# The second chunk's C product as seven block products, with its state sums made by accumulating transfers

## The chip, the cores and the metric

The kernel runs on one core of a Trainium2 chip. The time is the device time of one execution in microseconds (us). The kernel before took 206.87 us (median of three runs, 206.71 to 207.6). The engines are named as in the profile: PE is the tensor engine, DVE the vector engine, ACT the scalar engine, POOL is GpSimd and SP the sync engine, which only issues transfers here. POOL's transfers can add to their destination; SP's can only copy or transpose.

## The reference, cut to what matters

Two branches run on the same input `x` (2048 tokens x 640) and a gate mixes them:

```python
g = sigmoid((x * gate_w).sum(-1, keepdims=True))
# branch a: a diagonal complex state-space layer with 640 states
h_t = Lam_bar * h_(t-1) + x_t B_bar                  # a scan over the 2048 tokens
a   = 2 * (h Cmat).real + x * Dskip                  # the C product
# branch b: a dense layer pair
b   = gelu(x w1 + b1) w2 + b2                        # 640 -> 1728 -> 640
out = g * a + (1 - g) * b
```

The C product multiplies the real and the imaginary part of 640 states, so 1280 numbers a token, with a matrix of 1280 x 640.

## The kernel before

The 2048 tokens are four chunks of 512 (`CH`), and a chunk is four tiles of 128 tokens (`TPC`). Each chunk passes through four stages.

- `ff1(c)` makes x w1 + b1 and its gelu. PE fills a PSUM bank with five matmuls of 512 columns (line 305) and ACT evicts it into `gel[c]` (line 314).
- `ssm(c)` makes the input of the scan, x B: five matmuls of 512 columns for each of ten banks (line 481), which ACT evicts into `bu` buffers (line 484, eight buffers). DVE then runs, for each of the five groups of 128 states, a rotation (three operations of 128 x 1024), two scans (line 575), a rotation back (three operations, line 557) and writes the states into `hs[c]`. Between two chunks ACT turns the end states into the next start (`turn_carry`, four small activations, line 590).
- `fin_b(c)` is the w2 product. It is made as a product of 2 x 2 blocks with seven block products in place of eight (Strassen's scheme, in Winograd's form): tokens are halved, the 1728 inner rows are halved, and the 640 columns are halved. PE multiplies, and ACT copies a partial result to a second bank where two results share a first part (`fork`, line 744). ACT also scales each result by the gate into the f32 tiles `gb` (`out_of`, line 752). The sums of gelu blocks that the scheme needs are made by ACT's negated copies (`minus`, line 682) and POOL's accumulating transfers (`plus`, line 677). One product, Q, goes into both halves of a row of tiles; `twice` sends it from an f32 buffer `gq` (two buffers) with an accumulating transfer.
- The C product comes last and gives the output. Chunks 0 and 1 have it in the plain form, `fin_a` (line 812): for each of four tiles and two column halves, ten matmuls of 320 columns, 80 in all. The term x * Dskip is put into the bank by ACT before (`seed`, line 668), and one DVE operation (line 817) multiplies by the gate and adds `gb`. Chunks 2 and 3 have it as seven block products, `fin_s` (line 877): the tokens, the states (real and imaginary half) and the columns are halved, and seven products of two tiles and five matmuls make 70 matmuls. Its steps are X (first product), a copy X to Y, the Q product, then Y, X (with copies to Z and W) and Z. ACT makes the copies (line 883) and evicts Q into `gq` (line 920). DVE adds the skip term into `gb` (`skip_in`, lines 859 and 861), Q (`part_7`, line 904) and makes the outputs (`done`, line 892). For chunks 2 and 3 DVE also makes the four sums of state blocks (`h_sums`, line 836) into `M7`, `hs` itself, `M6` and `M3`. The sums of blocks of the matrix C (`U4` to `U7`) are made once, during `ff1(3)`, by ACT and POOL.

Seven products need the sums of states: with the blocks a, b (first half of the tokens) and g21, d (second half), M7 = a - g21, g21 becomes g21 + d, M6 = a - (g21 + d), M3 = b + M6.

The order on PE, ACT, POOL and SP is the order of the calls at the end of the kernel (lines 973 to 1015), with further work hung in by dictionaries of hooks. On DVE the order is made by a small planner: operations wait in a list and are let out by estimated times of PE, ACT and DVE (`dve_now`, `let_out`, `ck`). All engines run their lists in order, so an operation that waits holds up all that stand behind it. From chunk 1 on the calls are:

```python
gates(1); load_xT(2); load_skip(); fin_b(0, ...)
ff1(2, ...); gates(2); fin_a(0, sums(1)); load_xT(3)
ssm(2, ...); fin_b(1, ...); fin_a(1, ...); ssm(3)
ff1(3, ...); gates(3); fin_b(2, ...); fin_s(2, ...); fin_b(3, ...); fin_s(3, ...)
```

PSUM has eight banks, and `gel`, `hs`, `gq` and `g` have two buffers each.

Of the kernel before, what the change touches and what calls it, by code (L numbers as in the profile page):

```python
# [16 lines left out]
P = 128  # L17
# [25 lines left out]
def kernel(  # L43
# [41 lines left out]
    xT = [xA, xB, xB, xA]  # L85
# [12 lines left out]
    CT_im = const.tile([P, KS, D], BF16, name="CT_im")  # L98
    TCOS = const.tile([P, KS, CH], BF16, name="TCOS")
# [77 lines left out]
    tfi = work.tile([P, HC], I32, name="e", bufs=1)  # L177
    nc.gpsimd.iota(tfi[:], pattern=[[1, HC]], base=0, channel_multiplier=0)
# [8 lines left out]
    tf = const.tile([P, NP], F32, name="tf")  # L187
# [72 lines left out]
    nc.vector.tensor_copy(out=tf[:, NQ:NP], in_=tfi[:])  # L260
# [105 lines left out]
    scr = gelp.tile([P, KF * CH // 2], F32, name="gel")  # L366
# [21 lines left out]
    kk = work.tile([P, KS, NP], I32, name="bu", bufs=8)  # L388
# [27 lines left out]
    nc.vector.tensor_tensor(out=u, in0=tf[:].rearrange("p (o i) -> p o i", o=1).to_broadcast([P, KS, NP]), in1=over(thp_c[:], NP), op=ALU.mult)  # L416
# [59 lines left out]
    def inputs(c, ks):  # L476
        bu = work.tile([P, 2, CH], BF16, name="bu", bufs=8)
        for ri, BT in enumerate((BT_re, BT_im)):
            p = bank()
            for kd in range(KD):  # L480
                nc.tensor.matmul(p[:], lhsT=BT[ks >= KSA][:, kd, (ks % KSA if ks < KSA else ks - KSA) * P:][:, 0:P], rhs=xT[c][:, kd, :],  # L481
                                 start=(kd == 0), stop=(kd == KD - 1))
                pe(CH)
            nc.scalar.activation(out=bu[:, ri, :], in_=p[:], func=ACT.Identity)  # L484
            act(0.6)
        return bu, ck.act
# [157 lines left out]
    def gates(c):  # L644
        sl = slice(c * TPC, (c + 1) * TPC)

        def f():
            nc.vector.tensor_scalar(out=gcol[:, 0, sl], in0=gz[:, sl], scalar1=0.5, scalar2=0.5, op0=ALU.mult, op1=ALU.add)
            nc.vector.tensor_scalar(out=gcol[:, 1, sl], in0=gz[:, sl], scalar1=-0.5, scalar2=0.5, op0=ALU.mult, op1=ALU.add)
            nc.vector.tensor_scalar(out=gcol[:, 2, sl], in0=gz[:, sl], scalar1=0.5, scalar2=-0.5, op0=ALU.mult, op1=ALU.add)  # L650

        dve_now(ck.act + 0.3 if c > 0 else ck.pe, 0.2, f)
# [68 lines left out]
    def fin_b(c, at={}, gs=None):  # L721
# [59 lines left out]
        fork("X", "Z")  # L781
        if c < NCH - 1:
            part_7()
# [46 lines left out]
    U5, U7, U6, U4 = (narrow(t, KS * HD).rearrange("p (k d) -> p k d", k=KS) for t in (BT_re[1][:], BT_im[1][:], xB[:], w1b_sb[:]))  # L830
    M6, M7 = (t[:].rearrange("p k t -> p (k t)").rearrange("p (k t) -> p k t", k=KS) for t in (BT_im[0], BT_re[0]))
    M3 = narrow(xA[:], KS * HT).rearrange("p (k t) -> p k t", k=KS)
    C11, C12, C21, C22 = (t[:, :, h * HD:(h + 1) * HD] for t in (CT_re, CT_im) for h in range(2))

    def add(out, x, y, op):
        return lambda: nc.vector.tensor_tensor(out=flat(out), in0=flat(x), in1=flat(y), op=op)

    def h_sums(c):
        (a, b), (g21, d) = ([hs[c][:, i, r] for r in range(2)] for i in range(2))
        steps = []  # L840
        for out, x, y, op in ((M7, a, g21, ALU.subtract), (g21, g21, d, ALU.add), (M6, a, g21, ALU.subtract), (M3, b, M6, ALU.add)):
            steps.append(lambda fn=add(out, x, y, op): dve_now(0, 0.8, fn))
        return steps, (a, M7, M6, b, g21, M3, d), (C11, U7, U6, C21, U5, C22, U4)

    wide = [narrow(w1a_sb[:], 6 * D)[:, j * 2 * D:(j + 1) * 2 * D].bitcast(F32) for j in range(3)]
    wide += [xA[:].rearrange("p k t -> p (k t)")[:, KS * HT:].bitcast(F32), narrow(w1c_lo[:], 2 * D).bitcast(F32)]
# [8 lines left out]
    def skip_in(c, tiles, d0, d1, ready=0):  # L855
        for a in tiles:
            ti = c * TPC + a
            if a >= H:
                dve_now(ready, 0.82, lambda: nc.vector.tensor_tensor(out=gbs[ti][:], in0=gbs[ti][:], in1=GS[c][a - H], op=ALU.add))
                continue  # L860
# [4 lines left out]
    def fin_s(c, lhs, rhs, at={}):  # L865
# [104 lines left out]
    def sums(c):  # L970
# [17 lines left out]
    fin_a(0, sums(1))  # L988
    load_xT(3)
    ssm(2, {KS - 1: lambda: skips(1)})  # L990
    fin_b(1, seeds(1))
    fin_a(1, {**sums(2), 3: lambda: minus(U6, C22, 1.5)})
    ssm(3)
    gel_tile(3)
    nc.sync.dma_start(out=U7, in_=C12)
    steps, lhs, rhs = h_sums(2)
    ff1(3, 0, {1: lambda: (minus(U5, C11, 1.5), plus(U7, U6), plus(U5, C12), plus(U6, U5)),
               5: lambda: (skips(2), let_out(0, 2), [f() for f in steps[:3]]),
               7: lambda: (skips(2, H), [load_xn((NCH - 1) * TPC + H + j, narrow(w1a_sb[:], 6 * D)[:, (4 + j) * D:(5 + j) * D]) for j in range(H)]),
               10: lambda: (nc.sync.dma_start(out=U4, in_=C21), plus(U4, U6))})  # L1000
    for a, t in ((0, w1c_hi[:].rearrange("p k f -> p (k f)")[:, 0:D]), (1, xB[:].rearrange("p k t -> p (k t)")[:, KS * HD:KS * HD + D])):
        load_xn((NCH - 1) * TPC + a, t)
    gates(3)
    nc.vector.tensor_scalar(out=gcol[:, 3, NT - 2 * TPC:NT], in0=gcol[:, 0, NT - 2 * TPC:NT], scalar1=-1.0, scalar2=None, op0=ALU.mult)
# [4 lines left out]
    last, lhs3, _ = h_sums(3)  # L1009
    fin_s(2, lhs, rhs, {0: lambda: skip_in(2, (0, 1), HD, D, ck.act + 0.5), 1: lambda: (minus_d(3), skips(3))})  # L1010
    fin_b(3, {0: lambda: (let_out(1e9), [f() for f in last]),
# [3 lines left out]
    fin_s(3, lhs3, rhs)  # L1015
# [30 lines left out]
```

## Time and profile before

| | |
|---|---|
| time, median of three runs | 206.87 us |
| the profiled execution | 206.56 us, of which the span from first to last instruction is 204.8 us |
| PE busy | 200.6 us (98%), 1301 matmuls |
| DVE busy | 186.6 us (91%) |
| ACT busy | 140.7 us (69%) |
| POOL busy | 50.6 us (25%) |
| chain that ended last | PE 97% |
| granted PE clock | 1.00 throughout |

The span is the time from the first to the last instruction; the execution is 1.8 us longer. The chain that ended last is followed back from the last instruction: at each step to what released it, or to the instruction before it on its engine. A share of 97% for PE says that nearly all of the time one matmul followed another. The stages stand in that chain with their starts: `ssm(2)` at 94.9 us, `fin_b(1)` at 105.7, `fin_a(1)` at 119.2, `ssm(3)` at 130.1, `ff1(3)` at 140.9, `fin_b(2)` at 155.5, `fin_s(2)` at 168.8, `fin_b(3)` at 178.4 and `fin_s(3)` at 191.7. Timeline rows give the start of an instruction in us from the span's start, its duration, engine, line, operation and tiles; a bracket at the end is the idle time before it and what ended that.

### The profile page before, as it was taken

What the parts mean: (1) busy time and instruction counts of PE and PEld (TensorE: products, weight loads), DVE (VectorE), ACT (ScalarE), POOL (GpSimd) and SP (SyncE); (2) the same over time, 40 slices, a digit from 0 to 9 for tenths busy, and PEclk for the clock granted to TensorE, in tenths of its full rate; (3) what the DMA queues carried; (4) which work ended last, traced back from release to release, by engine and by line L of the source; (5) the groups of instructions that cost most, each with busy time, mean ns of one, the idle gap of its engine ahead of it and who ended that gap; (6) DMA issues with size and microseconds to landing.
All of it is one profiled execution on the core that took longest, in us unless ns stands there. A gap on an engine that the chain in (4) does not pass through costs nothing.

```text
span 204.8 us, 3592 instructions
## 1 busy us (share of the span) xinstructions
PE 200.6 (98%) x1301; PEld 119.3 (58%) x1301; DVE 186.6 (91%) x314; ACT 140.7 (69%) x271; POOL 50.6 (25%) x83
## 2 busy tenths in 40 slices
PE   8999999999999999999999999999999999999993
PEld 5744544454477544675457777544446777777762
DVE  2799999999999999999999999999999999686573
ACT  4696856997866799991764899266776699255520
POOL 8506930313330410031001052200412170124000
PEclk9999999999999999999999999999999999999999
DMA  6999999999999160159932369912596989719303
GB/s 192 193 144 223 194 303 158 203 224 287 177 210 219 23 109 15 50 104 239 194 90 53 74 120 234 235 35 80 89 190 121 182 159 198 175 24 208 60 0 128
DMA packets 45190, 30.28 MB, mean 148 GB/s; under 512 B 26898, under 2 KB 42612, under 8 KB 45172
## 3 DMA queue, kind: packets, MB, share of 16 engines
q0 software_dynamic: 6448, 12.53, 36.1%
q1 hardware_dynamic: 38148, 17.03, 35.5%
q10 hardware_dynamic: 576, 0.49, 0.7%
q8 instruction: 10, 0.16, 0.3%
q14 instruction: 8, 0.07, 0.1%
HBM read 7.79 MB, written 2.62 MB: 51 GB/s over the span
## 4 chain that ended last, share of the span: by engine, by line
PE 97%; DVE 1%; DVEq 0%; issue 0%
PE bank L305 28%; PE bank L732 26%; PE bank L481 21%; PE bank L812 11%; PE bank L877 9%; PE bank L264 1%; PE bank L329 1%; DVE ot L892 0%; PE bank L267 0%; DVE xA L274 0%; DVEq L1041 0%; PE bank L408 0%; PE bank L420 0%
## 5 line engine op out<-in xcount | busy, mean ns | idle before, releaser
L314 ACT ACTIVATE gel<-bank,colB 128x512 bf16<-128x512 f32 (+1 forms) x52 | 33.5, 692 | 7.9 <-PE bank L305 7.6
L575 DVE TENSOR_TENSOR_SCAN g<-r_c,carry,v 128x512 bf16<-128x512 f32 x30 | 38.3, 1277 | 0.0
L484 ACT ACTIVATE bu<-bank 128x512 bf16<-128x512 f32 x40 | 23.3, 600 | 19.3 <-PE bank L481 19.2
L732 PEld LDWEIGHTS <-gel 128*128 128x128 bf16 x280 | 27.3, 98 | 11.1 <-issue 0.2
L732 PE MATMUL bank<-w_sb,gel 128*128 128x320 bf16 x168 | 24.3, 299 | 0.0
L752 ACT ACTIVATE gb<-bank,gcol 128x320 f32<-128x320 f32 x32 | 16.2, 526 | 7.4 <-PE bank L732 6.9
L305 PEld LDWEIGHTS <-w1a_sb 128*128 128x128 bf16 x162 | 13.9, 98 | 12.0 <-issue 0.2
L812 PEld LDWEIGHTS <-hs 128*128 128x128 bf16 x160 | 15.6, 98 | 6.0
L481 PEld LDWEIGHTS <-BT_im 128*128 128x128 bf16 x100 | 9.7, 98 | 12.0 <-DMA BT_im<-in_A_B_im_dram 0.5
L481 PEld LDWEIGHTS <-BT_re 128*128 128x128 bf16 x100 | 9.6, 98 | 11.0
L744 ACT ACTIVATE bank<-bank 128x320 f32<-128x320 f32 x16 | 6.8, 423 | 11.0 <-PE bank L732 11.0
L305 PE MATMUL bank<-xA,w1a_sb 128*128 128x128 bf16 (+2 forms) x102 | 14.1, 291 | 0.0
L557 DVE TENSOR_TENSOR v<-wa,bu 128x1024 bf16<-128x1024 bf16 x20 | 13.7, 685 | 0.1
L557 DVE TENSOR_TENSOR hs<-wb,g 128x1024 bf16<-128x1024 bf16 x20 | 13.7, 685 | 0.1
L557 DVE TENSOR_TENSOR g<-TSIN,g 128x1024 bf16<-128x1024 bf16 x20 | 13.7, 685 | 0.1
L557 DVE TENSOR_TENSOR wb<-TCOS,g 128x1024 bf16<-128x1024 bf16 x20 | 13.7, 686 | 0.0
L557 DVE TENSOR_TENSOR bu<-TSIN,bu 128x1024 bf16<-128x1024 bf16 x20 | 13.6, 682 | 0.1
L812 PE MATMUL bank<-CT_re,hs 128*128 128x320 bf16 x80 | 13.5, 299 | 0.0
L812 PE MATMUL bank<-CT_im,hs 128*128 128x320 bf16 x80 | 13.5, 299 | 0.0
L732 PEld LDWEIGHTS <-N 128*128 128x128 bf16 x112 | 11.0, 98 | 4.3
L557 DVE TENSOR_TENSOR wa<-TCOS,bu 128x1024 bf16<-128x1024 bf16 x20 | 13.4, 670 | 0.0
L305 PEld LDWEIGHTS <-w1b_sb 128*128 128x128 bf16 x80 | 7.7, 98 | 9.6 <-DMA w1b_sb<-in_B_w_dram 0.7
(193 smaller groups left out, 398.1 us busy)
## 6 DMA issues: line engine op xcount, KB each, us to landing
out_dram<-ot SPq DMA_DIRECT2D x15, 160.0 KB, 5.0
w_sb<-in_B_w_dram SPq DMA_DIRECT2D x4, 480.0 KB, 5.7
gel<-N POOLq DMA_DIRECT2D x4, 448.0 KB, 4.9
N<-gel POOLq DMA_DIRECT2D x3, 448.0 KB, 5.6
gel<-gel POOLq DMA_DIRECT2D x3, 448.0 KB, 7.3
N<-N POOLq DMA_DIRECT2D x3, 448.0 KB, 5.2
gb<-gq POOLq DMA_DIRECT2D x4, 320.0 KB, 4.8
xn<-in_A_x_dram SPq DMA_DIRECT2D x8, 160.0 KB, 4.2
```

What stands on the lines that cost most here:

```text
L264: nc.tensor.matmul(pA[:, 0:n], lhsT=ones(P), rhs=ones(n), start=True, stop=True)
L305: nc.tensor.matmul(p[:, t0:t1], lhsT=w, rhs=xT[c][:, kd, t0:t1], start=(kd == 0) if first is None else first, stop=(kd == last), skip_grou ...
L314: nc.scalar.activation(out=dst, in_=src, func=ACT.Gelu_apprx_tanh, bias=b1_c[p0:p1, kf:kf + 1])
L481: nc.tensor.matmul(p[:], lhsT=BT[ks >= KSA][:, kd, (ks % KSA if ks < KSA else ks - KSA) * P:][:, 0:P], rhs=xT[c][:, kd, :], start=(kd == 0 ...
L484: nc.scalar.activation(out=bu[:, ri, :], in_=p[:], func=ACT.Identity)
L557: nc.vector.tensor_tensor(out=o, in0=a, in1=b, op=op)
L575: nc.vector.tensor_tensor_scan(s["g"][:, ri, :], r_c[:, ks:ks + 1].to_broadcast([P, CH]), s["v"][:, ri, :], init, ALU.mult, ALU.add)
L732: nc.tensor.matmul(p[:, 0:HD], lhsT=lhs[:, s, j * P:(j + 1) * P], rhs=rhs[:, s, :], start=fresh and s == 0, stop=s == KH - 1, skip_group_c ...
L744: nc.scalar.activation(out=quad[j][dst][:, 0:HD], in_=quad[j][src][:, 0:HD], func=ACT.Identity)
L752: nc.scalar.activation(out=gbs[ti][:, h * HD:(h + 1) * HD], in_=quad[j][name][:, 0:HD], func=ACT.Identity, scale=gcol[:, 1, ti:ti + 1])
L812: nc.tensor.matmul(p[:, 0:d1 - d0], lhsT=hs[c][:, a // H, j // KS, j % KS, (a % H) * P:][:, 0:P], rhs=CT[:, j % KS, d0:d1], start=False, s ...
L877: nc.tensor.matmul(t[j][:, d0:d1], lhsT=A[i][:, k, j * P:(j + 1) * P], rhs=B[i][:, k, d0:d1], start=fresh and k == 0, stop=k == KS - 1, sk ...
```

## The change

Chunk 1's C product becomes `fin_s(1)`: 70 matmuls in place of 80, the seven products, four bank copies of two, and two Q evictions on ACT. Its eight seeds on ACT go, and its skip term goes to `skip_in` on DVE (four operations of 320 columns, two of 640), with two `part_7`.

The state sums of chunk 1 are not made on DVE: `sum_7` and `sum_6` let ACT write -g21 into `M7` and `M6` (now tiles of their own) and let POOL add a, d and a to `M7`, `g21` and `M6`. `M3` of chunk 1 lies in the gelu buffer of chunk 1; SP copies b into it and POOL adds `M6`.

The sums of C's blocks are needed earlier. `U7` is C12 in place, to which POOL adds -C22 right after `fin_a(0)`. `U6` lies in `xA`: ACT writes -C22 there during `fin_a(0)` and, as the first operation of `fin_b(1)`, -C11; POOL then adds `U7`. `U5` and `U4` of chunk 1 lie in `N3` and `N2`, the buffers of `fin_b(1)`: SP copies C22 and C21 there when the products that read `N3` and `N2` are done, and POOL adds `U6` (and `M6` to `M3` in between). Chunks 2 and 3 get their `U5` and `U4` the same way in `ff1(3)`.

A new hook, `hook(4)`, stands in `fin_b` between the copy X to Z and `part_7`. The x of chunk 3 is loaded into `xB`, after `ssm(2)`, and no longer into `xA`. The `bu` buffers are six in place of eight. Two small tiles of the setup move into the scratch part of a gelu buffer. The fourth gate column is made in `gates` for chunks 1 to 3. The plain loads of chunk 2's x (`load_xn`) stand after `fin_s(1)`.

```diff
-    xT = [xA, xB, xB, xA]
+    xT = [xA, xB, xB, xB]
+    M6, M7 = (const.tile([P, KS, HT], BF16, name=n) for n in ("M6", "M7"))
...
-        bu = work.tile([P, 2, CH], BF16, name="bu", bufs=8)
+        bu = work.tile([P, 2, CH], BF16, name="bu", bufs=6)
...
+            if c > 0:
+                nc.vector.tensor_scalar(out=gcol[:, 3, sl], in0=gz[:, sl], scalar1=-0.5, scalar2=-0.5, op0=ALU.mult, op1=ALU.add)
...
         fork("X", "Z")
+        hook(4)
         if c < NCH - 1:
             part_7()
...
+    U7, U6 = C12, block(xA)
+    U54 = {1: (block(N3), block(N2)), 2: (block(BT_re[1]), block(BT_im[1]))}
+    U54[3] = U54[2]
+    def M3(c):
+        home = gel[1][:, 0, 0:KH, :] if c == 1 else xB[:]
+        return narrow(home, KS * HT).rearrange("p (k t) -> p k t", k=KS)
...
+    def sum_7():
+        (a, _), (g21, d) = state(1)
+        minus(M7[:], g21, 1.25)
+        plus(flat(M7[:]), flat(a))
+        plus(flat(g21), flat(d))
+
+    def sum_6():
+        (a, b), (g21, _) = state(1)
+        minus(M6[:], g21, 1.25)
+        plus(flat(M6[:]), flat(a))
+        nc.sync.dma_start(out=flat(M3(1)), in_=flat(b))
+
+    def sums_54(c, first=lambda: None):
+        U5, U4 = U54[c]
+        nc.sync.dma_start(out=U5, in_=C22)
+        nc.sync.dma_start(out=U4, in_=C21)
+        plus(U5, U6)
+        first()
+        plus(U4, U6)
...
-    fin_a(0, sums(1))
-    load_xT(3)
-    ssm(2, {KS - 1: lambda: skips(1)})
-    fin_b(1, seeds(1))
-    fin_a(1, {**sums(2), 3: lambda: minus(U6, C22, 1.5)})
-    ssm(3)
+    fin_a(0, {**sums(1), 3: lambda: minus(U6, C22, 1.5)})
+    plus(U7, U6)
+    ssm(2, {2: sum_7, KS - 1: lambda: (skips(1), skips(1, H))})
+    load_xT(3)
+    fin_b(1, {0: lambda: (minus(U6, C11, 1.5), plus(U6, U7)),
+              1: sum_6,
+              4: lambda: sums_54(1, lambda: plus(flat(M3(1)), flat(M6[:]))),
+              3: lambda: skip_in(1, (0, 1), 0, HD)})
+    fin_s(1, {0: lambda: skip_in(1, (0, 1), HD, D, ck.act + 0.5)})
+    for a in range(TPC):
+        load_xn(2 * TPC + a)
+    ssm(3, {1: lambda: minus_c(2), 3: lambda: minus_d(2)})
     gel_tile(3)
-    nc.sync.dma_start(out=U7, in_=C12)
...
-    ff1(3, 0, {1: lambda: (minus(U5, C11, 1.5), plus(U7, U6), plus(U5, C12), plus(U6, U5)),
+    ff1(3, 0, {1: lambda: sums_54(2),
```

## The prediction, made before the changed kernel ran

> **What bounds the kernel now.** I read the page first: busy shares, then the chain that ended last.
>
> ```profile
> span 204.8 us, 3592 instructions
> ...
> PE 200.6 (98%) x1301; PEld 119.3 (58%) x1301; DVE 186.6 (91%) x314; ACT 140.7 (69%) x271; POOL 50.6 (25%) x83
> ...
> PE 97%; DVE 1%; DVEq 0%; issue 0%
> ```
>
> PE is the bound: what takes a matmul away gains, and any idle PE is lost for good. Then the chain in order of time around the change:
>
> ```profile
> 105.70 1.90 PE bank L732 x14
> 107.60 0.02 issue
> 107.62 11.57 PE bank L732 x84
> 119.19 10.87 PE bank L812 x80
> ...
> 168.80 9.61 PE bank L877 x70
> ```
>
> 80 plain matmuls take 10.87, 70 block matmuls 9.61. And after the first 14 matmuls of `fin_b(1)` PE stood 0.02: it waited for the copy X to Y. So I read ACT's timeline there, then POOL's, the transfers' landing times, DVE's tail and PE's.
>
> ```profile
> 106.60 0.65 ACT L590 ACTIVATE carry<-e,e,cq 128x1 f32<-128x1 bf16 x2
> 107.16 0.90 ACT L744 ACTIVATE bank<-bank 128x320 f32<-128x320 f32 x2
> ...
> 125.20 1.52 ACT L682 ACTIVATE xB<-CT_im 128x1600 bf16<-128x1600 bf16 x1
> 126.63 0.28 ACT L590 ACTIVATE e<-e,nsL 128x1 f32<-128x1 bf16 x1
> ```
>
> The copies start at 107.16, right after the carry, with no idle before: PE got its bank just in time. A 1600-wide copy moves ACT on by 1.43 (125.20 to 126.63).
>
> ```profile
> 109.98 0.86 POOL L677 DMA_DIRECT2D gel<-N  x1 [15.38 <-PE bank L732]
> 118.30 2.43 POOL L677 DMA_DIRECT2D gb<-gq  x2 [7.46 <-ACT gb L752]
> ```
>
> ```profile
> gel<-N POOLq DMA_DIRECT2D x4, 448.0 KB, 4.9
> ...
> gel<-gel POOLq DMA_DIRECT2D x3, 448.0 KB, 7.3
> ...
> w1a_sb<-gq POOLq DMA_DIRECT2D x2, 320.0 KB, 5.0
> ...
> BT_re<-CT_re POOLq DMA_DIRECT2D x1, 400.0 KB, 7.4
> w1b_sb<-CT_im SPq DMA_DIRECT2D x1, 400.0 KB, 3.2
> ...
> w1c_lo<-gq POOLq DMA_DIRECT2D x1, 320.0 KB, 6.7
> ```
>
> The last column is us from issue to landing. POOL idles between those two issues; the change fills this stretch.
>
> ```profile
> 176.41 1.23 DVE L892 SCALAR_TENSOR_TENSOR ot<-bank,gcol,gb 128x320 bf16<-128x320 f32 x2 [1.76 <-PE bank L877]
> ...
> 197.19 1.23 DVE L892 SCALAR_TENSOR_TENSOR ot<-bank,gcol,gb 128x320 bf16<-128x320 f32 x2
> ```
>
> ```profile
> 198.48 1.57 PE L877 MATMUL bank<-CT_im,xA 128*128 128x320 bf16 x10
> ```
>
> DVE, without idle from 100 on, first waits 1.76 for PE before 176.41. In `fin_s(3)` the product X3 overwrites the bank from which DVE makes an output: the second operation at 197.19 ends at 198.42, PE goes on at 198.48.
>
> **The change part by part.** The sum is made against the profiled execution, 206.56, 0.31 under the median 206.87.
>
> *Matmuls.* 10.87 - 9.61 = 1.26 gained.
>
> *ACT at the head of `fin_b(1)`.* Negating C11 into `U6` now stands between the carry and the copies X to Y. ACT can't be earlier: the carry follows the last `bu` eviction, which PE paces (105.74). So the copies start 1.43 later and PE's Y product too: 1.43 lost. Bounds: 0 if ACT had that much slack (the 0.02 row says no), 1.5 if the strided source costs more. I take 1.43. Behind the negation wait both copies and the Y evictions. ACT's negation into `M7`, 1280 wide, is hidden: ACT idles 0.48 before each `bu` eviction, so it has caught up three evictions later, and seven other banks stand free. Negating C22 falls into 4.4 us of ACT idle after 91.7.
>
> The Trainium skill's Perfetto Trace Analysis, section Optimizing Scalar/DVE Operations, says that with DVE saturated it may make sense to offload work to ACT. By it ACT's added work would cost 0 here and the total be 1.43 less; the 107.16 row decides against it.
>
> *POOL and SP, and who waits for them.* POOL now issues, in this order: M7, g21, U6, b += N2 (as before), M6, U5, M3, U4, and only then the two gb<-gq that stood at 118.30. SP's copy of C21 into `N2` must wait until b += N2 has landed, and U4's add waits for that copy. The Q evictions of `fin_s(1)` write the same two `gq` buffers, so on ACT they wait until both gb<-gq have landed; behind them stand a carry and the copies X to Z, and behind these PE's X5 product.
>
> When is X5 due? `fin_s(1)` starts at 119.03 + 1.43 = 120.46; in `fin_s(2)` X5 stands 5.48 after the start (168.64 to 174.12), so 125.94. When can it start? b += N2 issues at 109.98 + 1.43 = 111.41. With each transfer at its own row: +4.9 landed, +3.2 copied, +0.55 and +0.96 for POOL's issues of U4 and the first gb, +5.0 landed: 126.0. Then Q eviction 0.44, carry 0.93 (106.23 to 107.16), copy 0.42: 127.8, a stall of 1.85. But these rows had few transfers beside them. Here, from 108.6 on: 400 + 448 + 320 + 400 + 320 + 400 + 320 + 400 + 400 + 640 = 4048 KB (4.15 MB), where the busiest stretches moved 197 and 243 GB/s (120 to 126 and 126 to 132, DMA share 1.10 and 1.07): 17.1 to 21.0 us, to 125.7 at best and 129.6 at worst. With each of the three landings half-way to its slowest kin row (4.9 and 7.3, 3.2 and 7.4, 5.0 and 6.7): 130.2. I take the middle of 126.0 and 130.2, 128.1, because both rows fit in part: a stall of 4.0. Ends: 1.85, and with all three at the slowest row 134.3, a stall of 10.2. A gain has no way in: PE only waits.
>
> The Trainium skill's DMA: Bandwidth & Descriptors, section Issuing engines are not separate DMA queues, says that transfers of all issuers share the same 16 engines and interleave, so spreading these over SP and POOL buys no bandwidth; its section Bandwidth gives 341 GB/s for 1 MB. At that figure 4.15 MB would be an estimated 12.2 us, landing times alone would decide, and the total would be 209.9; the 197 to 243 of this trace make it later.
>
> *DVE's load.* Added before 173: four `skip_in` of 0.46, two of 640 columns and two `part_7` of about 0.95 (0.88 busy and the wait for the result), 5.6 in all; the state sums of chunk 1 were never on DVE, and the outputs keep number and price. Together with 0.9 of waits for PE in `fin_s(1)`, DVE's chunk-3 work falls some 6 to 8 us behind. Listing its new order with the spacings of the old rows, DVE reaches the X3 output of `fin_s(2)` with 1.3 to spare: the wait at 176.41 absorbs most of the lag, the rest is moved behind. After the outputs of `fin_s(2)` now stand eight operations of chunk 3 (two 0.60, scan 1.19, 0.60, scan 1.31, 0.73, 0.73, 0.61: 6.4) and one of 0.60 between the outputs, all of them before the four state sums. From 176.41 to the end of the X5 output was 22.0, of which DVE idled about 5.5 (0.46, 1.93, 1.12, 0.76, 0.69, and 0.6 between rows); now it is 22.0 - 5.5 + 7.0 = 23.5. X3 of `fin_s(3)` starts 1.4 later. The state sums themselves are in time (M7 ends at 190.9 for a Q product at 193.1, on the clock without the middle stall). Ends: 0.9, if DVE's short waits stay shorter, and 3, if the 1.3 of slack isn't there. I take 1.4.
>
> *At nothing.* Six `bu` buffers: the tightest reuse (chunk 2's fifth, written at 104.66) takes one that DVE read last at 82.9. x of chunk 3 now loads after 105.7 instead of 96.95: SP is held 5.65, landing 6.7, so by 118 for a need at 130. It delays SP's M3 copy to 111.4, needed at 127. ACT's negation into `M6` (1.2, between the Y evictions and the copies X to Z) waits for g21's landing: issued about 102.5, 7.3 later 109.8, while ACT comes there at 111.6 and PE needs the copies at 114; 2.9 more of landing time would show. The four plain loads of chunk 2's x stand behind four output stores on SP and land about 141.7 for DVE's 145.9 (on the clock without the middle stall). Gate columns add two operations of 0.07. The eight seeds that leave ACT (0.4 each) free nothing that PE waited for. Without these covers each would cost its own time, at most a few us for the loads.
>
> Sum: 206.56 - 1.26 + 1.43 + 4.0 + 1.4 = 212.1.
>
> **The rivals.**
>
> *Transfers land as their rows say* (the share of DMA in 108 to 120 is only 0.18 to 0.46 now, which speaks for it; the 4 MB against): stall 1.85, total 210.0. Chance 0.17, for 209 to 210.9.
>
> *Transfers choke*: the landings go to the slowest rows, and b += N2, issued at 111.41 and read at 117.13 + 1.43 = 118.56, is late too. Stall 10.2: 218.3. For: six transfers in flight at once. Chance 0.22, for 213.7 to 218.3.
>
> *The middle wait never binds*: both gb<-gq land by 124.1. The chain would need 12.7 for what its own rows put at 14.6. 206.56 - 1.26 + 1.43 + 1.4 = 208.1. Chance 0.06.
>
> *Faster*: the released matmuls are all that counts. Place: PE's queue after 105.7; price: 1.26; it decides as long as PE's added idle stays under that. 205.3. For: PE is 97% of the chain; against: the copies at 107.16 had no slack, and that alone costs 1.43. Chance 0.04; another 0.03 for a total within 0.5%.
>
> **How the numbers follow.** 0.5% (1.0 us) is about what a measurement of this kernel can tell from no change. The forecast, 210.9 to 213.7, has 0.48; its value, 212.1, is the prediction. 208.5 to 216.5 takes in the forecast, the first rival, most of the second, and half of the third, 0.8 or a little more. Faster 0.04, same 0.03, slower 0.93.
>
> **What would show it.** In the changed profile: `fin_s(1)` with 70 matmuls; PE idle of about 1.4 after the first 14 matmuls of `fin_b(1)`, released by ACT's copy; ACT idle in front of `fin_s(1)`'s first Q eviction, ended by a gb<-gq landing, and PE idle before X5; DVE without idle from about 177 to 200, and PE idle of about 1.4 before X3 of `fin_s(3)`, released by DVE. Wrong it would be if landings stretch less or more than I think, or if ACT reaches the copies by another way.

## The result, and the profile after

The changed kernel takes 218.75 us (median of five runs) against 207.22 us for the kernel before, run beside it: 1.0556 times as long, 95% interval 1.0536 to 1.0576. The profiled execution took 218.73, its span 216.9. The forecast was 212.1, its range 208.5 to 216.5: slower was right, the size was not. Executions more than 1.5% above the fastest of the same kernel (here one of the six, 226.84) are left out of all totals and ratios.

The page of the changed kernel, its span, its busy times and the shares of its chain:

```profile
span 216.9 us, 3601 instructions
...
PE 201.3 (93%) x1291; PEld 119.7 (55%) x1291; DVE 191.7 (88%) x324; ACT 142.3 (66%) x273; POOL 56.4 (26%) x89
...
PE 76%; DVE 10%; DMA 6%; ACT 4%; issue 2%; POOL 1%; DVEq 0%; POOLq 0%; ACTq 0%
```

PE has ten matmuls fewer and is yet busy 0.7 longer, and its share of the chain fell from 97% to 76%. PE's timeline shows where: the first row of `fin_b(1)`, the rows before which PE stood idle, the two after the long wait, and the first row of `ssm(3)`. (A name such as X5 below is a block product: number 5, added into bank X.)

```profile
105.76 2.06 PE L735 MATMUL bank<-w_sb,gel 128*128 128x320 bf16 x14
109.27 2.06 PE L735 MATMUL bank<-w_sb,gel 128*128 128x320 bf16 x14 [1.45 <-ACT bank L747]
...
134.85 2.83 PE L912 MATMUL bank<-N,hs 128*128 128x320 bf16 x10 [8.57 <-ACT bank L918]
137.47 1.91 PE L912 MATMUL bank<-CT_im,gel 128*128 128x320 bf16 x10
139.22 1.52 PE L912 MATMUL bank<-N,hs 128*128 128x320 bf16 x10
140.57 1.24 PE L482 MATMUL bank<-xB,BT_re 128*128 128x512 bf16 x5
...
210.85 1.52 PE L912 MATMUL bank<-CT_im,xB 128*128 128x320 bf16 x10 [1.66 <-DVE ot L927]
```

Four losses: 1.45 before the Y product of `fin_b(1)`, 8.57 before X5 of `fin_s(1)`, then the products X5 and X3 themselves, which start 2.62 and 1.75 before the next in place of 1.36 (1.65 together), and 1.66 before X3 of `fin_s(3)`. They close the account. The first rows of `fin_b(1)` and of `ssm(3)` in the kernel before:

```profile
105.54 4.15 PE L732 MATMUL bank<-w_sb,gel 128*128 128x320 bf16 x28
...
129.90 1.24 PE L481 MATMUL bank<-xA,BT_re 128*128 128x512 bf16 x5
```

From the start of `fin_b(1)` to that of `ssm(3)` the kernel before took 129.90 - 105.54 = 24.36, so 23.10 without the 1.26 of the ten matmuls. Now it is 140.57 - 105.76 = 34.81, which is 11.71 more: 1.45 + 8.57 + 1.65 = 11.67. From there to `fin_s(3)` nothing differs (61.66 before, 61.67 now), `fin_s(3)` up to its last product is 1.64 longer, the stages ahead of `fin_b(1)` 0.22.

The middle wait, in the chain in order of time (start, duration, what it was):

```profile
117.91 5.20 DMA N<-CT_im
...
123.67 0.51 POOL N L680
124.20 0.74 POOL gb L680
124.94 8.10 DMA gb<-gq
...
133.12 0.44 ACT gq L955
133.56 0.36 ACT e L591 x2
133.92 0.56 ACT carry L591 x2
134.48 0.33 ACT bank L918
134.85 5.89 PE bank L912 x30
```

This is the route that the forecast named, link by link: SP's copy of C21 into `N2`, U4's addition waiting for it on POOL, the two gb<-gq behind that, then Q eviction, carry and X-to-Z copy on ACT, then PE. ACT's own rows name the shared buffer and the copy's place:

```profile
107.38 1.52 ACT L685 ACTIVATE xA<-CT_re 128x1600 bf16<-128x1600 bf16 x1
108.80 0.73 ACT L747 ACTIVATE bank<-bank 128x320 f32<-128x320 f32 x2
...
131.36 0.44 ACT L955 ACTIVATE gq<-bank 128x320 f32<-128x320 f32 x1 [8.64 <-DMA gb<-gq]
133.12 0.44 ACT L955 ACTIVATE gq<-bank 128x320 f32<-128x320 f32 x1 [1.33 <-DMA gb<-gq]
```

The granted clock says what slowed X5 and X3. In a table by stretches the last three columns are granted PE clock, DMA share and GB/s:

```profile
126.00:132.00 6.00, 0.28 (x3) 0.07 (x1) 1.90 (x3) 0.44 (x1) 0.99 (x1) 0.95 1.11 181
132.00:138.00 6.00, 3.15 (x12) 1.76 (x12) 0.00 (x0) 2.71 (x9) 0.00 (x0) 0.50 0.05 8
138.00:144.00 6.00, 6.00 (x35) 3.38 (x34) 4.96 (x9) 1.80 (x6) 0.00 (x0) 0.98 0.16 55
```

In stretches of 1 us the clock is 0.71 from 131 to 132 and 0.87 from 138 to 139, and 0.50 between them: PE was granted half its clock from about 131.4, while it still stood idle, to about 138.3.

### The profile page after: what moved, and what is told of

Same layout as the page of the kernel before. It is cut to its first block, busy times and chain, and to the rows that moved or that the text cites. A ratio compares the mean times of both kernels' runs of the same rounds, so it can differ in the third digit from the quotient of the medians.

```text
span 216.9 us, 3601 instructions
## 1 busy us (share of the span) xinstructions
PE 201.3 (93%) x1291; PEld 119.7 (55%) x1291; DVE 191.7 (88%) x324; ACT 142.3 (66%) x273; POOL 56.4 (26%) x89
## 3 DMA queue, kind: packets, MB, share of 16 engines
HBM read 7.79 MB, written 2.62 MB: 48 GB/s over the span
## 4 chain that ended last, share of the span: by engine, by line
PE 76%; DVE 10%; DMA 6%; ACT 4%; issue 2%; POOL 1%; DVEq 0%; POOLq 0%; ACTq 0%
PE bank L307 26%; PE bank L482 20%; PE bank L735 15%; PE bank L912 7%; PE bank L816 5%; DMA gb<-gq 4%; DMA N<-CT_im 2%; DVE ot L927 2%; DVE gb L939 2%; PE bank L266 1%; PE bank L331 1%; DVE g L576 1%; DVE gb L893 1%; DVE gb L895 1%; DVE M L845 1%
## 5 line engine op out<-in xcount | busy, mean ns | idle before, releaser
L485 ACT ACTIVATE bu<-bank 128x512 bf16<-128x512 f32 x40 | 22.6, 600 | 14.3 <-PE bank L482 14.2
L927 DVE SCALAR_TENSOR_TENSOR ot<-bank,gcol,gb 128x320 bf16<-128x320 f32 (+2 forms) x25 | 12.6, 532 | 14.0 <-PE bank L912 13.2
L307 PEld LDWEIGHTS <-w1a_sb 128*128 128x128 bf16 x162 | 14.4, 101 | 12.0
L912 PEld LDWEIGHTS <-hs 128*128 128x128 bf16 x125 | 12.4, 101 | 13.9 <-issue 8.8
L307 PE MATMUL bank<-xB,w1a_sb 128*128 128x512 bf16 x90 | 19.9, 379 | 0.0
L482 PE MATMUL bank<-xB,BT_re 128*128 128x512 bf16 x75 | 18.6, 379 | 0.0
L482 PE MATMUL bank<-xB,BT_im 128*128 128x512 bf16 x75 | 18.6, 379 | 0.0
L482 PEld LDWEIGHTS <-BT_im 128*128 128x128 bf16 x100 | 9.8, 98 | 11.8
L307 PE MATMUL bank<-xB,w1b_sb 128*128 128x512 bf16 x60 | 13.4, 379 | 0.0
```

The costliest lines, as they stand in the source:

```text
L307: nc.tensor.matmul(p[:, t0:t1], lhsT=w, rhs=xT[c][:, kd, t0:t1], start=(kd == 0) if first is None else first, stop=(kd == last), skip_grou ...
L912: nc.tensor.matmul(t[j][:, d0:d1], lhsT=A[i][:, k, j * P:(j + 1) * P], rhs=B[i][:, k, d0:d1], start=fresh and k == 0, stop=k == KS - 1, sk ...
L927: dve_now(ck.pe + 0.2, 0.54, lambda: nc.vector.scalar_tensor_tensor(out=ots[ti][:, o + d0:o + d1], in0=t[j][:, d0:d1], scalar=gcol[:, 0, t ...
```

## The experiments

"Stage" below is the time from `fin_b(1)`'s start to `ssm(3)`'s (the start of Z4 plus 1.36), and "lost" is what it has over 23.10. Stages are compared because `fin_b(1)` starts anywhere between 105.7 and 108.3 in the profiles of the changed kernel and its variants (once, in run 13, at 115.05). Stage, lost and last wait are read from the one profiled execution of each run; in runs 3 and 4 that one took 220.47 and 212.87, 1.3 below and 2.4 above the total in the table.

| run | total, us | ratio to before (95%) | stage | lost | last wait of PE in `fin_s(3)` |
|---|---|---|---|---|---|
| changed kernel | 218.75 | 1.0536 to 1.0576 | 34.81 | 11.71 | 1.66 |
| 1 own Q buffers | 208.77 | 1.0066 to 1.0108 | 25.02 | 1.92 | 1.65 |
| 2 gb<-gq first | 211.36 | 1.0188 to 1.0236 | 27.46 | 4.36 | 1.30 |
| 3 negation behind the copies | 221.81 | 1.0673 to 1.0761 | 35.92 | 12.82 | 1.65 |
| 4 runs 1 and 3 | 210.47 | 1.0145 to 1.0191 | 26.53 | 3.43 | 1.65 |
| 5 DVE's order | 207.30 | 0.9974 to 1.0034 | 24.74 | 1.64 | none |
| 6 less in the tail | 207.77 | 0.9986 to 1.0052 | 24.97 | 1.87 | 0.34 |
| 7 U6 early | 211.96 | 1.0179 to 1.0270 | 28.11 | 5.01 | 1.66 |
| 8 runs 7 and 5 | 210.03 | 1.0060 to 1.0154 | 28.04 | 4.94 | none |
| 9 changed kernel, x late | 221.90 | 1.0647 to 1.0769 | 37.47 | 14.37 | 1.66 |
| 10 run 7, x late | 210.03 | 1.0074 to 1.0179 | 26.00 | 2.90 | 1.66 |
| 11 run 8, x late | 208.68 | 1.0016 to 1.0088 | not used | | |
| 12 run 5, x late | 210.10 | 1.0057 to 1.0198 | not used | | |
| 13 changed kernel, no x | 217.76 | 1.0446 to 1.0562 | 32.98 | 9.88 | 1.66 |
| 14 run 7, U6 behind b | 209.78 | 1.0055 to 1.0155 | 24.13 | 1.03 | 1.66 |
| 15 run 8, U6 behind b | 206.75 | 0.9956 to 1.0013 | 24.03 | 0.93 | none |

### The shared buffers

Run 1 gives `fin_s(1)`'s Q evictions another place; run 2 keeps the buffers and changes POOL's order.

```diff
-            q[j] = fwork.tile([P, HD], F32, name="gq", bufs=2)
+            q[j] = fwork.tile([P, HD], F32, name="gq", bufs=2) if c > 1 else flat(gel[1][:, 1, KH:2 * KH, :])[:, j * 2 * HD:(j + 1) * 2 * HD].bitcast(F32)
```

> The changed kernel with one line altered: in fin_s(1) the Q evictions go into the d block of chunk 1's gelu tile, which nothing reads any more, in place of the two gq buffers that the transfers gb<-gq of fin_b(1) still read. Nothing else moves on any engine. Theory (the two shared gq buffers are the 8.57 us wait, and the 1.65 us that the next 20 matmuls lost at a lower granted clock is a consequence of that idle): X5 then waits for U5 alone, which was issued at 121.06 and lands 4.9 later at 126.0, where X5 is due at 126.1; M3 (121.6 + 5.5 = 127.1) and U4 (123.7 + 4.9 = 128.6) are due at 127.5 and 128.9. PE idle before X5 at most 0.5, the granted clock full there, total 218.7 - 8.6 - 1.65 = 208.5, up to 209. DVE loses the idle in which it caught up, so the wait before X3 of fin_s(3), 1.66 now, may grow by 0 to 2: 208.5 to 211. Rival (the 4 MB of transfers are the limit whichever buffer is asked for): U5, M3 and U4 land as late as the two gb<-gq did, 7 to 8 after issue, so 128.3 to 131.5: a stall of 2 to 4 in two places remains, with a clock loss: 212 to 214.

```diff
         fork("X", "Z")
-        hook(4)
+        settle()
...
             twice(gbs[c * TPC + H + j][:], gq[j])
-        hook(3)
+        at.get(4, lambda: None)(), hook(3)
```

> The changed kernel with the order of issues on POOL altered: the two gb<-gq of fin_b(1) stand ahead of the additions U5, M3 and U4 and not behind them; DVE, ACT, PE and SP keep their order. Theory (the 8.57 us are the landing of the two gb<-gq, and 3.8 of it the place in POOL's queue): they are issued when ACT's last gb eviction of Z is done, about 119.5 and 120.4 in place of 124.2 and 125.1, and land 7.2 and 8.0 later, 126.7 and 128.4. Behind it 0.44 + 0.93 + 0.42 for eviction, carry and copy: X5 at 130.2 against 126.1 due, a stall of about 4.1, less clock loss than 1.65 because the idle is shorter: 212.5 to 214.5. Rival (the transfers together are the limit): the last of five transfers lands when it did, now U4 in place of gb<-gq, and X5, X3 or Z4 wait as long: 217 to 219.

Run 1: 208.77, and PE's rows from X5 on are without any wait but a small one before Z4:

```profile
126.03 1.52 PE L912 MATMUL bank<-N,hs 128*128 128x320 bf16 x10
...
129.33 1.52 PE L912 MATMUL bank<-N,hs 128*128 128x320 bf16 x10 [0.42 <-DMA N<-xA]
```

10.0 us go with one buffer name, the lost clock with them. The same two transfers still take 7.4 to land; nobody waits for them. So U5, M3 and U4 were not what PE waited for, but for 0.42, and the rival falls. In run 2 the evictions wait far less, as ACT's rows show, and so does PE before X5:

```profile
125.52 0.44 ACT L955 ACTIVATE gq<-bank 128x320 f32<-128x320 f32 x1 [2.02 <-DMA gb<-gq]
127.16 0.44 ACT L955 ACTIVATE gq<-bank 128x320 f32<-128x320 f32 x1 [1.20 <-DMA gb<-gq]
```

```profile
129.22 1.52 PE L912 MATMUL bank<-N,hs 128*128 128x320 bf16 x10 [2.16 <-ACT bank L918]
```

The stall before X5 is 2.16 (4.1 was expected: the two landed in 5.7 and 6.5 and not in 7.2 and 8.0, and were issued 13.15 after the stage's start, 0.6 earlier than assumed), X5 runs at full clock, and the total is 211.36: below the expected 212.5 to 214.5. Both runs together show that the stall is the landing of gb<-gq, and that most of it comes from their place in POOL's queue.

### The copy ahead of X to Y

Run 3 moves one ACT instruction behind the two copies; run 4 adds run 1 to it.

```diff
-        fork("X", "Y")
+        fork("X", "Y"), at.get(5, lambda: None)()
...
-    fin_b(1, {0: lambda: (minus(U6, C11, 1.5), plus(U6, U7)),
+    fin_b(1, {5: lambda: (minus(U6, C11, 1.5), plus(U6, U7)),
```

> The changed kernel with one ACT instruction moved by two: at the head of fin_b(1) the negation of C11 into U6 stands behind the two copies X to Y. Theory (1.45 us is that negation on ACT's queue): the idle after the first 14 matmuls of fin_b(1) goes from 1.45 to 0.1 or less. The transfers behind follow PE's Y product, which is earlier by as much, and U6's is at most 0.7 later, so the middle wait stays within 0.7 of 8.57: 217.3, up to 218. Rival (the transfers in flight set the end of the middle wait whatever PE does before): the middle stall grows by what the first one loses, and the total stays at 218.7.

> Both alterations together: Q evictions of fin_s(1) into the gelu tile and the negation of C11 behind the copies X to Y. Theory: 218.7 - 8.6 - 1.65 - 1.45 = 207.0 with 1.66 of it still the tail's wait on DVE; the transfers U5, M3 and U4 are now the next to be late (X5 due 1.45 earlier, at 124.7, U5 landing between 125 and 126), which gives back 0.3 to 1.5, and the tail may grow since DVE no longer has an idle stretch: 207.0 to 210. Rival (the sums of the parts don't add, because the transfers are the limit): 211 or more.

The 1.45 went: 28 matmuls of `fin_b(1)` run without a break. Yet both kernels got slower, by 3.1 and 1.7: run 3 above its rival, run 4 between its theory and its rival. PE's row of run 3:

```profile
136.87 2.83 PE L912 MATMUL bank<-N,hs 128*128 128x320 bf16 x10 [10.98 <-ACT bank L918]
```

POOL's rows of run 3 show what came instead:

```profile
110.71 1.50 POOL L680 DMA_DIRECT2D xA<-CT_re  x1 [5.76 <-ACT xA L685]
111.57 1.57 POOL L680 DMA_DIRECT2D gel<-N  x1
112.71 1.32 POOL L680 DMA_DIRECT2D M<-hs  x1
123.12 0.86 POOL L680 DMA_DIRECT2D N<-xA  x1 [9.09 <-DMA N<-CT_im]
```

`U6`'s addition, b += N2 and M6 now stand on top of each other, with 0.9 and 1.1 between their issues (2.4 and 1.7 in the changed kernel). M6 lands after 9.1 in place of 7.1, and U5, for which POOL waits until C22's copy has landed (the bracket of its row), is issued 16.67 after the stage's start in place of 15.30 (121.06 - 105.76). My theory said that the transfers would follow PE's earlier Y product; it fell, and the rival's "no gain" was still too kind.

### The tail

Both changes to run 1. Run 5 makes the planner put DVE's operations in another order, run 6 leaves out most of the skip term of the first half of chunk 3.

```diff
-            dve_now(ck.pe + 0.2, 0.54, lambda: nc.vector.scalar_tensor_tensor(
+            dve_now(ck.pe + (2.4 if c == 2 and t is X and not j else 0.2), 0.54, lambda: nc.vector.scalar_tensor_tensor(
...
-                skip_in(c, (H + j,), 0, D, ck.pe)
+                skip_in(c, (H + j,), 0, D, ck.pe + (2.4 if c == 1 else 0))
```

> The kernel with its own place for the Q evictions (208.77), and DVE's order altered in two places by later ready times for the planner: two operations of chunk 3's recurrence stand ahead of the skip additions of fin_s(1), where DVE idled 1.2 for gb<-gq, and four more (0.6 + 0.6 + 0.6 + 1.2 = 3.0) stand ahead of the X3 outputs of fin_s(2), where DVE idled 0.7 for PE, and no longer behind the outputs. Theory (DVE is level with PE at the X3 outputs of fin_s(2); only what it has to do from there on sets when it makes the X5 outputs of fin_s(3), for which PE waits 1.65): DVE leaves that point about 1.0 later and with 3.0 less to do, so the last wait falls to 0 to 0.4; total 207.1 to 207.5. Rival (the late outputs of fin_s(2) hold banks that fin_b(3) needs, or DVE is behind all along): the 1.65 stays or moves to fin_b(3): 208.5 to 209.5.

```diff
-              3: lambda: skip_in(3, (0, 1), 0, HD)}, GS[3])
+              3: lambda: skip_in(3, (0, 1), 0, 2)}, GS[3])
...
-    skip_in(3, (0, 1), HD, D)
+    skip_in(3, (0, 1), HD, HD + 2)
```

> The kernel with its own place for the Q evictions (208.77), leaving out most of chunk 3's skip term in its first half: four DVE operations of 0.46, between the state sums and the outputs of fin_s(3), work on 2 columns in place of 320. The order is the same. Theory (DVE's work between the X3 outputs of fin_s(2) and the X5 outputs of fin_s(3) is what PE waits 1.65 for): 4 x about 0.38 less, the wait falls to 0.1 to 0.3, total 207.2 to 207.4. Rival (the wait is for something else than DVE's load, such as the gq transfers): 208.8.

Run 5: no wait is left in `fin_s(3)`, 207.30. Run 6: 0.34 is left, so 1.3 us less of DVE work took 1.3 us from the wait; 207.77, a little above the expected 207.2 to 207.4. DVE's rows of run 1 and of run 5 around the X3 outputs of `fin_s(2)`, run 1 first:

```profile
175.84 0.68 DVE L558 TENSOR_TENSOR bu<-TSIN,bu 128x1024 bf16<-128x1024 bf16 x1
177.20 0.55 DVE L927 SCALAR_TENSOR_TENSOR ot<-bank,gcol,gb 128x320 bf16<-128x320 f32 x1 [0.69 <-PE bank L912]
```

```profile
177.18 1.28 DVE L576 TENSOR_TENSOR_SCAN g<-r_c,carry,v 128x512 bf16<-128x512 f32 x1
178.38 0.99 DVE L927 SCALAR_TENSOR_TENSOR ot<-bank,gcol,gb 128x320 bf16<-128x320 f32 x2
```

In run 1 DVE is level with PE here and waits 0.69 (1.43 in the changed kernel, where the long stall let it catch up); what is queued behind this point sets the end, and the last wait is the same 1.65 in both. In run 5 the scan and three more stand ahead of the outputs, and DVE has that much less to do afterwards.

### U6 early, and the load of x

Run 7 is run 1 with C11 negated in ACT's idle time at the end of `fin_a(0)` (the negation of C22 goes to `M6` and to free columns of `xA`), and with U6's addition issued as soon as `U7` is there. Run 8 adds DVE's order of run 5.

```diff
-    fin_a(0, {**sums(1), 3: lambda: minus(U6, C22, 1.5)})
-    plus(U7, U6)
-    ssm(2, {2: sum_7, KS - 1: lambda: (skips(1), skips(1, H))})
+    T22 = ((M6[:].rearrange("p k t -> p (k t)").rearrange("p (k d) -> p k d", d=HD), 0, 4), (xA[:].rearrange("p k t -> p (k t)")[:, KS * HD:KS * HD + HD].rearrange("p (k d) -> p k d", d=HD), 4, 5))
+    fin_a(0, {**sums(1), 3: lambda: ([minus(t, C22[:, a:b, :], 0.3 * (b - a) + 0.05) for t, a, b in T22], minus(U6, C11, 1.5))})
+    for t, a, b in T22:
+        plus(U7[:, a:b, :], t)
+    ssm(2, {2: lambda: (sum_7(), plus(U6, U7)), KS - 1: lambda: (skips(1), skips(1, H))})
...
-    fin_b(1, {0: lambda: (minus(U6, C11, 1.5), plus(U6, U7)),
-              1: sum_6,
+    fin_b(1, {1: sum_6,
```

> The kernel with its own place for the Q evictions (208.77), and C11's negation into U6 moved to the end of fin_a(0), where ACT idles 2.9 us; the negation of C22 that had that place goes into M6 and 320 free columns beside U6 instead, so U7's addition becomes two transfers. U6 += U7 is issued behind the additions M7 and g21 as soon as U7 has landed, near 105 in place of 109. Theory after the first four runs (the copy's place on ACT costs 1.45, and U6's transfer issued late, on top of b += N2 and C22's copy, is what delays U5, M3 and U4): no idle after the first 14 matmuls of fin_b(1), U5, M3 and U4 land 1.5 or more earlier in relation to PE than where the negation stood behind the copies, so X5, X3 and Z4 wait 0.4 at most together. From fin_b(1)'s start to ssm(3)'s start 23.1 to 23.6 in place of 25.0; total 206.9 to 207.4 with the tail's 1.65 unchanged. Rival (the DMA engines are full from 102 on, so an earlier issue lands no earlier): the waits in fin_s(1) stay at the 2.7 of the run with both alterations, total 209 to 210.5.

> Both of these: U6 early and DVE's new order. Theory: 208.77 less 1.45 and 0.4 in the middle and 1.65 in the tail: 205.3, which is the kernel before less the 1.26 of the ten matmuls; 0.3 to 0.7 more if a little of a wait stays: 205.3 to 206. Rival (with the waits gone DVE, busy for 191 us, is the bound, and PE's earlier start only makes it wait longer for DVE): 206.7 or more, with PE idle released by DVE.

Both theories failed, by 4.6 and 4.0 above the upper ends of what they expected. In run 7 PE waits 3.01 inside `fin_b(1)`, where the longest wait so far was 0.17 (run 3), and in run 8 it waits 3.00; run 7's row first:

```profile
121.20 3.43 PE L735 MATMUL bank<-w_sb,gel 128*128 128x320 bf16 x14 [3.01 <-DMA gel<-N]
```

```profile
121.07 2.08 PE L735 MATMUL bank<-w_sb,gel 128*128 128x320 bf16 x14 [3.00 <-DMA gel<-N]
```

The stretches of run 7 and its DMA issues near 106 to 113 (KB each, us from issue to landing):

```profile
111.00:114.00 3.00, 3.00 (x24) 2.16 (x23) 2.96 (x6) 1.74 (x3) 1.66 (x2) 1.00 1.73 78
114.00:117.00 3.00, 3.00 (x24) 2.16 (x23) 3.00 (x5) 2.57 (x9) 0.00 (x0) 1.00 1.48 141
```

```profile
gel<-N POOLq DMA_DIRECT2D x1, 448.0 KB, 10.3
xA<-CT_re POOLq DMA_DIRECT2D x1, 400.0 KB, 11.5
...
xB<-in_A_x_dram SPq DMA_TRANSPOSE x1, 11.8
```

U6's addition (issued 106.24) and the transposing load of chunk 3's x (106.64) run side by side, and both take twice their time: U6 11.5 where it took 6.0 in the changed kernel, x 11.8 where it took 5.4 to 5.5, and the core moves 78 GB/s in 111 to 114, at a DMA share of 1.73. Runs 9 to 12 put that load behind SP's three copies, run 9 in the changed kernel and the others in runs 7, 8 and 5.

```diff
-    load_xT(3)
...
               3: lambda: skip_in(1, (0, 1), 0, HD)})
+    load_xT(3)
     fin_s(1, {0: lambda: skip_in(1, (0, 1), HD, D, ck.act + 0.5)})
```

> The changed kernel with one transfer moved in SP's queue: the transposing load of chunk 3's x (640 KB, issued at 105.95) stands behind the copies for M3, C22 and C21, so it is issued near 117. Nothing else moves. Theory (the accumulating transfers of fin_b(1) stretch because that load shares the DMA engines with them: 112 to 126 stand between b += N2 and the last landing): b += N2 lands in about 5 in place of 6.3, C22's copy in 5 to 6 in place of 7.9, so U5 and U4 are issued 2 earlier and the two gb<-gq with them; the middle wait falls from 8.57 to 5 to 7, total 215 to 217.5. x must land by 138 for ssm(3), and does. Rival (the load only takes its turn, and the chain waits for the sum of all transfers anyway): 218.7 within 0.7.

> The kernel with its own place for the Q evictions and U6 early (211.96), with the load of chunk 3's x moved behind the copies for M3, C22 and C21 on SP. Theory (that load, issued at 106.6 together with U6 += U7, is what made U6 take 11.5, b += N2 10.3 and C22's copy 12.2, at 78 GB/s in 111 to 114 with the DMA engines busy throughout): U6 lands in 6 to 7, b += N2 in 5 to 6 and no longer holds PE's last product of fin_b(1) for 3.0, U5, M3 and U4 are issued from 119 on: fin_b(1) to ssm(3) 23.1 to 24, total 206.9 to 208 with the tail's 1.65. x, issued near 117, must land by 129: with 8 to 12 us it is just in time, or costs up to 1. Rival (the accumulating transfers choke each other): 210.5 or more.

> The same with DVE's new order, which takes away the tail's 1.65. Theory: 205.3 if nothing waits in the middle, 206.4 with a wait of 1 for x. Rival: 209 or more, as U6 early and DVE's order gave without moving the load (210.03).

> The kernel with its own place for the Q evictions and DVE's new order (207.3), with the load of chunk 3's x moved behind the copies on SP and the negation of C11 left at the head of fin_b(1). Theory: PE still waits 1.45 for that negation; the 0.3 before Z4 goes, so 206.7 to 207.2, unless the later x makes ssm(3) wait, up to 1 more. Rival (x, issued near 118 among five accumulating transfers, lands after 130): 208 or more.

None of the four is near its theory's total: run 9 lies above its theory and its rival, runs 10 and 11 between the two, and run 12 where its rival put it (208 or more). The load moved the trouble with it. In run 10 the transfers that it left behind land at the speed hoped for: U6 in 5.0, b += N2 in 4.4, M6 in 6.1. Those that it joined do not, as the issues of run 10 from 117 on show:

```profile
N<-xA POOLq DMA_DIRECT2D x2, 400.0 KB, 9.6
gb<-gq POOLq DMA_DIRECT2D x2, 320.0 KB, 10.6
gel<-M POOLq DMA_DIRECT2D x1, 320.0 KB, 10.1
```

In the changed kernel these are 4.1 and 5.7, 7.6, and 5.5. So in run 9 the same gb<-gq take 9.9 and the middle wait grows to 10.5. The expectation that the load only needed to be out of the way of b += N2 was wrong; in neither of the two places tried, 106 and 117, is it alone.

Two questions were left: how much of the 8.57 is due to that load, and whether U6 was slow because of it. Run 13 is the changed kernel without the load; runs 14 and 15 are runs 7 and 8 with U6's addition behind b += N2.

```diff
-    load_xT(3)
```

> The changed kernel leaving out the transposing load of chunk 3's x (640 KB): its recurrence works on chunk 2's x, which is still in that tile. All else, the shared gq buffers included, as in the changed kernel. Theory A (the load stretches the accumulating transfers beside it): b += N2, issued at 111.6, lands in 4.5 to 5 in place of 6.3, C21's copy in 3.5 to 4.5 in place of 5.2, U4 is issued near 120.5 to 121.5 and the two gb<-gq behind it land in 5 to 6.5 each in place of 7.2 and 8.0: by 127 to 129. With 0.44 + 0.93 + 0.42 behind it X5 starts near 129 to 130.5 against 126.1 due: a stall of 3 to 4.5, near the 4.0 that was forecast, with little clock loss: total 212 to 214. Theory B (the accumulating transfers stretch each other): stall 7 to 8.5, total 216.5 to 218.7.

```diff
-    ssm(2, {2: lambda: (sum_7(), plus(U6, U7)), KS - 1: lambda: (skips(1), skips(1, H))})
+    ssm(2, {2: sum_7, KS - 1: lambda: (skips(1), skips(1, H))})
...
-    fin_b(1, {1: sum_6,
+    fin_b(1, {1: lambda: (plus(U6, U7), sum_6()),
```

> The kernel with its own place for the Q evictions and C11 negated early (211.96), with U6 += U7 issued on POOL behind b += N2 (near 111) in place of ahead of it (106.2). The load of chunk 3's x stands at 106.6 as there. Theory (it was U6's transfer beside that load that made both slow, 78 GB/s in 111 to 114): by 111 the load has nearly landed; U6, b += N2, C22's copy and M6 land in 5 to 8 each, U5 is issued by 119 to 121: fin_b(1) without waits, X5, X3 and Z4 wait 0 to 2 together, total 207 to 209 with the tail's 1.65. Rival (a later U6 is late by itself): U5 is issued after 123 as in the run with both alterations, 2.7 or more of waits: 210 or more.

> The same with DVE's new order, which takes away the tail's 1.65. Theory: 205.3 to 207.3. Rival: 208.3 or more.

Run 13 took 217.76, 1.0 less than the changed kernel. Its profiled execution reached `fin_b(1)` 9 us later than the others, so only lengths inside the stage are read from it. PE's row before X5, and POOL's:

```profile
142.50 2.82 PE L912 MATMUL bank<-N,hs 128*128 128x320 bf16 x10 [6.93 <-ACT bank L918]
```

```profile
127.87 0.86 POOL L680 DMA_DIRECT2D N<-xA  x1 [4.36 <-DMA N<-CT_im]
...
132.61 0.86 POOL L680 DMA_DIRECT2D N<-xA  x1 [2.01 <-PE bank L912]
133.15 2.80 POOL L680 DMA_DIRECT2D gb<-gq  x2
```

b += N2 lands in 5.1 and U5 goes out 2.5 earlier, but then C21's copy, issued at 126.16, has U5 and M3 beside it: U4 is issued 132.61 - 126.16 = 6.4 later, in place of 123.67 - 117.91 = 5.8 in the changed kernel. The two gb<-gq take 6.3. The load was worth 1.0 (by the totals) to 1.6 (by the stall); the other 7 us of the stall remain without it, in the chain of copies and additions. My theory A, 3 to 4.5, falls; theory B, 7 to 8.5 and 216.5 to 218.7, holds for the total and nearly for the stall (6.93). Which of the additions slow each other was not separated.

Runs 14 and 15 behave as the theory said in the stage, and run 15's total lies in its expected range: no wait in `fin_b(1)`, and of `fin_s(1)`'s products only Z4 waits more than 0.2. PE's row of Z4 in run 15:

```profile
128.50 1.52 PE L912 MATMUL bank<-N,hs 128*128 128x320 bf16 x10 [0.64 <-DMA N<-xA]
```

So it was U6 beside the load, not a later U6, that cost 4 of the 5 us lost in run 7: the same instructions in another order on one queue lose 1.0 (run 14) and 0.9 (run 15) in place of 5. Run 14's median lies 0.8 above its expected 207 to 209; its runs spread from 208.16 to 210.66, and the profiled one began `fin_b(1)` at 108.33, 2.5 later than run 15's. Why the part ahead, which both share, takes longer in some executions was not looked into. Run 15 is the best kernel found: 206.75, 0.9984 of the kernel before, interval 0.9956 to 1.0013. The seven products of chunk 1 then cost nothing; that they gain is not shown.

## Why the prediction was wrong, by its own steps

*Matmuls, 1.26 gained.* Right. In run 1 the stage is 25.02, and 23.10 + 1.45 + 0.42 is 24.97.

*ACT at the head of `fin_b(1)`, 1.43 lost.* Right: 1.45, with the bank copies at 108.80, 1.42 after the start of the 1600-wide copy. The Trainium skill's page Perfetto Trace Analysis (section Optimizing Scalar/DVE Operations), weighed there, says that with DVE saturated offloading to ACT may make sense. Taken as free of cost it would have had 0 here; the row decided rightly. What the step did not see is that removing this loss moves U6's transfer onto others: runs 3 and 4 lost more than the 1.45 they won.

*The middle stall, 4.0.* This is the step that failed: it measured 8.57. The route was right in every link, and so was its first half. The forecast's sum with each landing half-way to its slowest row had the first gb<-gq on its way at 124.3; POOL began to issue the two at 124.20. After that three things went wrong. The landing of gb<-gq was put at 5.85 half-way, from a row of 5.0 with two loads of 160 KB beside it and one of 6.7 with two additions; the second took 8.1 in the chain, with U5, M3 and U4 issued within the 4 us ahead of it: 2.25 more. It also left POOL at 124.94 and not 124.3, being the second of two: 0.6. And I averaged 130.2 with 126.0, the sum of the undisturbed rows, "because both rows fit in part": 2.1. Together 4.95, and ACT's eviction starts at 133.12 where the forecast's middle had 128.1. The sum by bytes failed too: it put the landing at 129.6 at worst, from rates of 197 to 243 GB/s, and the core moved 181 from 126 to 132. The trace of before had no row for this many transfers at once; there the slow end, 134.3, deserved the weight. With the clock's 1.65 and 0.26 more in the tail, the stall's 4.57 makes 6.5 of the 6.6 by which the profiled 218.73 lies above the forecast's sum.

*The choke rival, 218.3 at a stall of 10.2.* Nearest in its total, and half right in its mechanism: landings stretched, but b += N2 was not late for PE, and the stall was 8.57. The total came near by luck, through the clock's 1.65, a loss that no case contained.

*The clock.* Not foreseen: 1.65 on top. The Trainium skill's page TensorE: Matmul & The Clock Gate, section Part 1: The HAM clock gate (the "warmup" mystery), states that about 3.4 us of idle put the array at half its clock until it has been busy about as long again. The rows here agree in the main (0.50 granted after 8.57 idle, 2.62 in place of 1.36 for ten matmuls), but run 7 shows a slow stretch after 3.01 already (0.50 granted from 122 to 125). A stall forecast above 3 us should have carried that price; my own 4.0 should have.

*The tail, 1.4.* Right: 1.66, with the mechanism named. Runs 5 and 6 show that it is what DVE has queued behind the X3 outputs of `fin_s(2)`. The slack there was put at 1.3 without the middle stall; run 1 shows 0.69.

*Hidden at nothing.* The load of chunk 3's x was costed at nothing because it lands in time. It does, and it costs 1.0 to 1.6 through the transfers that it slows; the other items of that list show no wait. The start of `fin_b(1)` 0.22 later lies within what it varies by.

*Transfers share the same engines* (the Trainium skill's page DMA: Bandwidth & Descriptors, section Issuing engines are not separate DMA queues): run 7 agrees, since POOL's additions and SP's load slow each other; that it is the engines they share is not shown. The 341 GB/s of the same page's section Bandwidth, measured there on a 1 MB load from HBM, are not reached in any stretch shown here: 181 in the changed kernel's, 78 and 141 in run 7's, 223 in run 15's. The 209.9 worked out from it is the same sum as the first rival's 210.0.

## What to carry to other kernels

Before moving work from an engine to transfers, list for each tile buffer of a ring who still reads it when its next writer comes: one shared pair of buffers (1280 bytes a partition) turned a slow but unneeded landing into 10 of the 11.5 us lost here. Price a landing by what is issued within the few us ahead of it, not by its row in a quiet stretch, and when a stall of about 3 us or more on PE is possible, add the clock that it will lose. A wait removed at one place releases transfers into another's stretch: look at the queue order again before the gain is booked.

## What the runs showed of the hardware that was not expected

- An accumulating transfer on POOL's queue and the transposing load on SP's slow each other. Side by side in run 7 they take 11.5 and 11.8; the addition took 5.0 with the load moved away (run 10), the load 5.3 with the addition moved away (run 15). In 111 to 114 the core moved 78 GB/s in run 7, at a DMA share of 1.73, against 223 GB/s in run 15, where U6 is issued 4.6 later. What in the load does this (its small packets, its path) was not tried. The row of run 15:

```profile
111.00:114.00 3.00, 3.00 (x24) 2.15 (x22) 2.97 (x6) 1.30 (x3) 2.61 (x3) 1.00 0.99 223
```

- Idle PE and the clock: with 2.2 us of idle before X5 (run 2) the next ten matmuls start 1.49 before those that follow, with 6.9 to 11 us (runs 13, 3, 9 and the changed kernel) 2.61 to 2.62, and up to 2.5 for the ten after. At 3.0 both were seen: in run 7 the 14 matmuls after 3.01 took 3.22 in place of 1.90, in run 8 after 3.00 they took 1.91. So the limit lies near 3 us here, or depends on more than the length of the gap. The granted clock in stretches of 1 us speaks for the second: by it the half clock lasted an estimated 3.4 us in run 7 (121.7 to 125.2, so it began when PE was already at work again), 6.8 in the changed kernel and in run 13, and 10.2 in runs 3 and 9, near whole multiples of 3.4. That would fit a clock that is set anew every 3.4 us, by which the moment of a wait of 3 us decides whether it costs anything; no run here was made to show it.
- The same gb<-gq of 320 KB landed in 5.0 (kernel before, beside two loads of 160 KB), 6.1 (run 2), 6.3 (run 13), 7.4 (run 1), 7.6 (changed kernel), 9.0 (run 3) and 10.6 us (run 10), medians of two, by what was beside them.
